# Products with past states in the other quarters of TensorE, fixed PSUM banks, and the low words' top bits on ScalarE

## The chip, the cores and the metric

One core of a Trainium2 chip runs the whole program. The metric is the device time of one execution, in microseconds (us), as the median of several executions. An engine is named as in the profile: PE is TensorE's matmul, PEld its weight load, DVE is VectorE, ACT is ScalarE, POOL is GpSimd, SP is SyncE, which issues nearly all DMAs.

## The reference, cut to what matters

Three layers in a row. The first is a linear recurrence over 768 time steps for 4 batches of 8 heads of width 48; the second a mixture with 32 soft slots; the third a gated MLP whose weights come as float64.

```
for t in range(S):                                    # S = 768
    state = alpha[:, :, t, :, None] * state + k_t (x) v_t
    y[:, :, t] = q_t @ state
x = y as (3072, 384)
logits = x @ phi;  slots = softmax over tokens, x -> 8 experts (relu) -> back to tokens
out = (silu(x @ w_gate) * (x @ w_val)) @ w_out        # float64 weights, float32 result
```

## The kernel before, in words

**Groups.** Two heads sit side by side on the partitions (0 to 47 and 64 to 111). A unit is such a pair for one batch (16 units), and a group is half a unit, that is three chunks of 128 steps: 32 groups, numbered g, with h = 0 for the first half of a unit and h = 1 for the second. The recurrence is done by chunk: `scan_w` and `scan_p` make running products of alpha on VectorE (L307, L314), `scale` multiplies k and q by them on GpSimd (L325), `emit_s` makes the 128x128 score products (L353), `emit_masks` masks them (L360 on VectorE, L362 on ScalarE and L363 on GpSimd), `emit_kt` transposes k (L371, copied out by L374), `emit_dh` makes each chunk's addition to the state (L390), `emit_st` adds the state before it (L402) and scales it on ScalarE (L404), `emit_past` multiplies q by the state before the chunk (L420), and `emit_ip` adds the masked scores times v (L432), after which ScalarE copies the three chunks to `xt` in one instruction (L434). `emit_xt` and `emit_l` transpose `xt` for the slots (L462, copied by L466) and make the logits (L453). After each 8 groups a batch is complete and `slot_steps` puts its steps (`peak`, `exps`, `keep`, `e_tok`, `part`, `l_tok`, `c_norm`) into the groups that follow.

**Order.** The schedule is written by hand: each engine runs its instructions in the order of the program text. In the loop of `fast`, group g issues on PE: state products, scores of g + 1, state products, k transposes of g + 1, `emit_xt` and `emit_l` of g - 1, a slot step, `emit_past(g)`, `emit_dh(g + 1)`, `emit_ip(g)`. A float32 product is two PE instructions with a weight load each.

**Tiles of the array.** `emit_past` has 64 contraction rows and up to 64 output columns for each head: the first head uses rows and columns 0 to 63 of the array, the second 64 to 127. `emit_s` uses the two halves of the rows, `emit_dh` and `emit_ip` the two halves of the columns. PSUM banks come from a pool of three (`psm`, in turn), two for scores, and one each for y and the logits.

**Float64 weights.** A block of `wgv` or `wo` comes as pairs of 32-bit words. For `wgv`, in the loop, `conv_y` scales the high words as float32 on ScalarE (`to_f32_y`, L249) into a place `z_c`; `conv(0)` takes the top three bits of the low words on VectorE (`to_f32_z`, L253); `conv(1)` and `conv(2)` join both and put the sign back on VectorE (`to_f32_p` L257, `to_f32_s` L261). 24 such blocks are converted, one in a group, in 24 of the groups. Each raw block lies in one of two places, and the load of the block after next is issued by SP when `conv_y` and `conv(0)` have read it.

**Memory.** An arena of two areas, near (31600 floats for each partition) and far (19184), holds everything; `pump` loads the slot layer's weight blocks (1536 floats, 768 KB) ahead in it, paced by a credit of 840 floats a group while unit loads remain, into whatever space is free. After the loop come the expert products (L856, L914) and then the MLP (L1010, L1011, L1049).

Of the kernel before, what the change touches and what calls it, by code (L numbers as in the profile page):

```python
# [11 lines left out]
U32 = mybir.dt.uint32  # L12
AF = mybir.ActivationFunctionType
# [21 lines left out]
GV0, RATE = 1, 840  # L35
TINY = 2.0 ** -55
NEAR, ROUND = 31600, 19184
# [55 lines left out]
def attention_slots_mlp(ctx: ExitStack, tc: tile.TileContext, kq, at, vt, phi, w1, w2, wgv, wo, cst, out):  # L93
# [13 lines left out]
    phs = const.tile([112, NU, NSL], F32, name="phs")  # L107
# [6 lines left out]
    amm = const.tile([112, 2, B * NU], F32, name="amm")  # L114

# [25 lines left out]
    def program(general):  # L141
# [14 lines left out]
        z_c = [(ar.alloc(GP, 0), GP)]  # L156

        zn = {nm: [0] * n for nm, n in (("a", 4), ("p", 5), ("v", 4), ("w", 2), ("x", 2))}
        zsize = {"a": HW, "p": HB, "v": 288, "w": HW, "x": 384}
        for z in "a0 a1 p2 a2 p3 v0 w0 a3 p4 v1 w1 p0 v2 p1 v3 x0 x1".split():  # L160
            zn[z[0]][int(z[1])] = ar.alloc(zsize[z[0]], 1)
# [17 lines left out]
        def psm():  # L179
            return ps_m.tile([128, 512], F32, tag="m", name="m")  # L180
# [82 lines left out]
        def done_c():  # L263
            drop(z_c.pop())
            for o in z_g:
                drop((o, 2 * GP))
            few[1] = ar.alloc(few[2], 0)
# [7 lines left out]
        def conv_y():  # L275
            i = gvd[0]
            if i < NG and ("wgv", divmod(i, 4)) in have:
                gvy[i] = to_f32_y(view(have["wgv", divmod(i, 4)]))

        def conv(part):  # L280
            i = gvd[0]
            if i not in gvy:
                return
            n, p = divmod(i, 4)
            raw = view(have["wgv", (n, p)])
            if n not in gvb:
                gvb[n] = need(BLK)
            dst = view((gvb[n][0] + GP * p, GP))
            if part == 0:
                to_f32_z(dst, raw)  # L290
# [11 lines left out]
        def scan_w(g, between=lambda: None):  # L302
# [5 lines left out]
            between()  # L308
# [71 lines left out]

        def emit_dh(g):
# [4 lines left out]
            dps[g] = psm()  # L386
# [4 lines left out]

        dps = {}
# [15 lines left out]
        yps = {}  # L408


        def emit_past(g):
            n, h = sgs[g]
            q = view(qp[g], 112)
            yps[g] = ps_y.tile([128, 512], F32, tag="y", name="y")
            for c in range(3):
                cc = 3 * h + c
                o = slice(c * CH, (c + 1) * CH)
                for s in range(2) if cc else ():
                    p = slice(0, 64) if s == 0 else slice(64, 112)
# [4 lines left out]
        def emit_ip(g):  # L424
            n, h = sgs[g]
            v = view(vv[g]).rearrange("p (c e) -> p c e", e=96)
            ps = yps[g]
            for c in range(3):
                o = slice(c * CH, (c + 1) * CH)
                for s in range(2):  # L430
                    p = slice(0, 64) if s == 0 else slice(64, 112)
                    nc.tensor.matmul(ps[p, o], lhsT=v[:, c, 48 * s:48 * s + p.stop - p.start], rhs=smk[g, s][:, c], start=False, stop=True, skip_group_check=True)  # L432
            xt[g] = (z_x.pop(0), 384)
            nc.scalar.copy(view(xt[g], 112), ps[0:112, 0:384])  # L434
            del smk[g, 0], smk[g, 1], yps[g]
            release(vv.pop(g), z_v, g + 4)
# [8 lines left out]
        def emit_l(g):  # L445
# [5 lines left out]
            for j in range(3):  # L451
                t0 = j * CH
                nc.tensor.matmul(lps[b][32 * j:32 * j + 32, CH * h:CH * h + CH], lhsT=phs[:, u, :], rhs=x[:, t0:t0 + CH], start=(u == 0 and h == 0), stop=(u == NU - 1), skip_group_check=True)  # L453

        def emit_xt(g, between=lambda: None):
# [3 lines left out]
            ps = psm()  # L459
# [8 lines left out]
        def slot_steps(b):  # L468
# [33 lines left out]

            def part(between=lambda: None):
# [3 lines left out]
                for r in range(2):  # L507
                    if r:
                        between()
                    for u, p, w in pieces:  # L510
                        for j in range(3):
                            nc.tensor.matmul(ps[32 * j:32 * j + 32, 96 * u:96 * u + 96 * w], lhsT=st["et"][:, r, 32 * j:32 * j + 32], rhs=xtok[:, p:p + w, 3 * r + j, :], start=(r == 0 and u == 0), stop=(r == 1), skip_group_check=True)
# [64 lines left out]
        def fast():  # L577
            pump_units(4)
# [43 lines left out]
            for g in range(NSG):  # L622
                n, h = sgs[g]
                nxt = g + 1 < NSG

                emit_st(g, 1 - h)
                if GV0 < g and (g <= 8 or g % 8 not in (3, 4)):
                    conv_y()
                if g + 3 < NSG:
                    scan_w(g + 3, lambda: conv(0))  # L630
                    scan_p(g + 3)
                else:
                    conv(0)
# [17 lines left out]
                if g:  # L651
                    emit_l(g - 1)
                    release(xt.pop(g - 1), z_x, g + 1)
# [7 lines left out]
                emit_past(g)  # L661
# [20 lines left out]
                pump_units()  # L682
            for r in z_t:
# [449 lines left out]
def _arrays(q, k, v, alpha, moe_phi, moe_w1, moe_w2, moe2_w_gate, moe2_w_val, moe2_w_out):  # L1133
# [17 lines left out]
    ph = np.zeros((112, NU, NSL), np.float32)  # L1151
    pr = moe_phi.reshape(NU, 2, D, NSL)
    for s in range(2):
        ph[64 * s:64 * s + 48] = pr[:, s].transpose(1, 0, 2)
# [32 lines left out]
```

## Time and profile before

| | |
|---|---|
| median of 3 runs | 388.98 us (387.81 to 390.64) |
| the profiled execution's own time | 387.89 us |
| its span, first to last instruction | 386.2 us |
| mean granted TensorE clock | 0.993 |
| loop over the groups | from about 10 to 153 us of the span |
| expert products | about 158 to 186 us |
| MLP | about 186 to 386 us |
| busy: PE, PEld, DVE, ACT, POOL | 95%, 72%, 76%, 52%, 27% |

The profiled execution lies 1.1 us under the median of the runs. A page's busy share is a mean over the three stages, which have different limits, so a stage is read by its own window. PE's busy time counts the pipeline's length of each matmul, so the pace of PE is read from the distance between starts. SP's rows are issues of DMAs; the time in such a row is the issue alone.

### The profile page before, as it was taken

The page shows a single profiled execution, that of the slowest core. Times are in us where ns is not written, and L with a number is a line of the kernel's source. Part 1 is how long each engine was busy: PE and PEld are TensorE (multiplying, and loading weights), DVE is VectorE, ACT ScalarE, POOL GpSimd, SP SyncE. Part 2 cuts the span into 40 slices and gives each one's busy share as a digit, 9 for nine tenths or more (in the row PEclk, how much of TensorE's full clock was granted, in tenths as well). Part 3 has the DMA queues.
Part 4 walks back from the last instruction along what each step waited for, and adds up shares of the span by engine and source line. Part 5 has one row for each costly group of instructions (what it writes and reads, how often), then busy time and mean ns, then how long its engine had stood idle before and what let it go on. Part 6 is the DMA issues. An engine that isn't in the chain of part 4 may idle for free.

```text
span 386.2 us, 8613 instructions
## 1 busy us (share of the span) xinstructions
PE 368.8 (95%) x3308; PEld 277.0 (72%) x3309; DVE 292.4 (76%) x566; ACT 200.8 (52%) x468; POOL 102.4 (27%) x105
## 2 busy tenths in 40 slices
PE   7799999999999999999899999999999999999992
PEld 3577777776777776433478778888888888888781
DVE  6999899999999973306789977777677867977540
ACT  2366665665567455523467655455445446446441
POOL 3379666795587650011200000000000000000000
PEclk9999999999999999999999999999999999999997
DMA  8999999999899986899900013204204104112002
GB/s 276 354 300 343 374 342 316 321 342 338 281 369 361 304 286 217 345 367 413 351 2 0 3 48 111 68 28 126 74 1 153 50 23 153 38 36 82 3 2 90
DMA packets 28627, 74.25 MB, mean 192 GB/s; under 512 B 3216, under 2 KB 11648, under 8 KB 28576
## 3 DMA queue, kind: packets, MB, share of 16 engines
q1 hardware_dynamic: 28256, 73.27, 53.9%
q8 instruction: 28, 0.46, 0.5%
q10 hardware_dynamic: 272, 0.21, 0.2%
q14 instruction: 23, 0.19, 0.2%
q0 software_dynamic: 48, 0.13, 0.1%
HBM read 68.87 MB, written 4.72 MB: 191 GB/s over the span
## 4 chain that ended last, share of the span: by engine, by line
PE 73%; DVE 6%; DMA 3%; ACT 2%; issue 1%; DVEq 0%; ACTq 0%
PE m L1049 22%; PE acc L1049 11%; PE s L353 4%; PE y L432 4%; PE y L420 4%; PE s L1010 4%; PE s L1011 4%; DMA near<-w 3%; PE s L856 3%; PE m L402 3%; PE m L390 2%; PE m L371 2%; PE l L453 2%; PE m L462 2%; DVE near L1016 2%; DVE rnd L1024 1%
## 5 line engine op out<-in xcount | busy, mean ns | idle before, releaser
L1049 PE MATMUL m<-rnd 128*128 128x512 f32 x432 | 129.3, 389 | 0.0
L1049 PEld LDWEIGHTS m<-rnd 128*128 128x128 f32 x432 | 81.1, 188 | 16.8
L1013 ACT ACTIVATE near<-s 128x512 f32<-128x512 f32 x72 | 43.1, 598 | 79.1 <-PE s L1010 79.1
L1049 PE MATMUL acc<-rnd 128*128 128x512 f32 x216 | 81.1, 392 | 0.8 <-DVE rnd L905 0.8
L325 POOL TENSOR_TENSOR far<-far 112x384 f32<-112x384 f32 x61 | 74.5, 1239 | 9.7 <-DVE far L307 4.7
L1016 DVE TENSOR_TENSOR near<-near,s 128x512 f32<-128x512 f32 x72 | 49.3, 685 | 35.3 <-ACT near L1013 35.3
L1024 DVE TENSOR_TENSOR rnd<-near,rnd 128x512 fp32r<-128x512 f32 x72 | 49.4, 686 | 3.1 <-ACT rnd L1022 3.1
L1049 PEld LDWEIGHTS acc<-rnd 128*128 128x128 f32 x216 | 40.5, 188 | 10.2 <-DVE rnd L905 1.6
L1022 ACT CAST rnd<-near 128x512 fp32r<-128x512 f32 x72 | 44.2, 614 | 0.2 <-DVE near L1016 0.2
L404 ACT ACTIVATE far<-m,tots 112x48 f32<-112x48 f32 x80 | 24.2, 302 | 24.1 <-PE m L402 13.3
L307 DVE TENSOR_TENSOR_SCAN far<-far,r 112x388 f32<-112x388 f32 x32 | 30.8, 961 | 5.8 <-DMA far<-at 3.2
L353 PE MATMUL s<-far 64*128 64x128 f32 x384 | 30.5, 289 | 3.5 <-POOL far L325 3.5
L1120 DVE TENSOR_REDUCE amm<-near 112x1 f32<-112x768 f32 x32 | 30.3, 946 | 3.5 <-DMA near<-at 3.5
L363 POOL TENSOR_SCALAR_AFFINE_SELECT far<-far 128x384 f32<-128x384 f32 x32 | 21.7, 677 | 42.3 <-ACT far L362 42.3
L314 DVE TENSOR_TENSOR_SCAN far<-far,r 112x387 f32<-112x387 f32 x32 | 30.7, 959 | 1.1
L434 ACT COPY far<-y 112x384 f32<-112x384 f32 x32 | 15.3, 479 | 27.7 <-PE y L432 27.7
L353 PEld LDWEIGHTS s<-far 64*128 64x128 f32 x384 | 24.4, 187 | 6.1 <-POOL far L325 4.4
L432 PE MATMUL y<-far 128*48 128x128 f32 (+1 forms) x384 | 28.6, 274 | 0.0
L1010 PE MATMUL s<-rnd 128*128 128x512 f32 x72 | 28.3, 393 | 0.0
L1011 PE MATMUL s<-rnd 128*128 128x512 f32 x72 | 28.2, 391 | 0.0
L257 DVE SCALAR_TENSOR_TENSOR near<-near 128x384 uint32<-128x384 uint32 x36 | 21.3, 593 | 8.5 <-ACT near L249 7.6
L261 DVE SCALAR_TENSOR_TENSOR near<-near 128x384 uint32<-128x384 uint32 x36 | 24.5, 681 | 0.3
(163 smaller groups left out, 489.7 us busy)
## 6 DMA issues: line engine op xcount, KB each, us to landing
near<-w SPq DMA_DIRECT2D x18, 768.0 KB, 7.7
far<-kq SPq DMA_DIRECT2D x32, 384.0 KB, 5.3
far<-w SPq DMA_DIRECT2D x14, 768.0 KB, 5.6
near<-wgv SPq DMA_DIRECT2D x24, 384.0 KB, 5.9
far<-at SPq DMA_DIRECT2D x32, 194.0 KB, 5.2
near<-at SPq DMA_DIRECT2D x16, 339.1 KB, 3.4
far<-vt SPq DMA_DIRECT2D x32, 144.0 KB, 4.7
near<-wo SPq DMA_DIRECT2D x12, 384.0 KB, 7.9
```

Of the source, the lines that this page charges most:

```text
L307: nc.vector.tensor_tensor_scan(w[:, ::-1], a[:, ::-1], rst[:, ::-1], 0.0, ALU.mult, ALU.add)
L314: nc.vector.tensor_tensor_scan(a, a, rst[:, 0:387], 0.0, ALU.mult, ALU.add)
L325: eng.tensor_tensor(out=xv, in0=xv, in1=sv, op=ALU.mult)
L353: nc.tensor.matmul(sps[g][s][:, o:o + CH], lhsT=k[64 * s:64 * s + 64, t0:t0 + CH], rhs=q[64 * s:64 * s + 64, t0:t0 + CH], start=True, stop ...
L432: nc.tensor.matmul(ps[p, o], lhsT=v[:, c, 48 * s:48 * s + p.stop - p.start], rhs=smk[g, s][:, c], start=False, stop=True, skip_group_check ...
L1010: nc.tensor.matmul(pg, lhsT=swk[n][:, 128 * o:128 * o + 128], rhs=ctT[t % 4], start=True, stop=True)
L1011: nc.tensor.matmul(pv, lhsT=swk[n][:, 256 + 128 * o:256 + 128 * o + 128], rhs=ctT[t % 4], start=True, stop=True)
L1013: nc.scalar.activation(sg, pg, AF.Silu)
L1016: nc.vector.tensor_tensor(out=h_, in0=sg, in1=pv, op=ALU.mult)
L1022: nc.scalar.copy(hi, h_)
L1024: nc.vector.tensor_tensor(out=lo, in0=h_, in1=hi, op=ALU.subtract)
L1049: nc.tensor.matmul(p, lhsT=passes[j][0][:, sl], rhs=passes[j][1], start=(f == 0 and j == 0), stop=(f == NF - 1 and j == 2))
```

## The change

- `emit_past` and `emit_ip` swap their order, and `emit_past(g - 1)` moves into group g, behind its first state products. The products with v now open the accumulation, and those with the past state close it; ScalarE's copy to `xt` follows `emit_past`.
- For the middle chunk of a group (`swap`), both put the first head's result on partitions 64 to 111 and the second's on 0 to 63, in another bank. So its products with the past state use the two quarters of the array that the outer chunks leave free. The copy to `xt` becomes two instructions. A second copy of phi with the heads exchanged, and an access pattern that reads the two heads in reverse (`x_rows`), undo the exchange further on.
- In the loop the three pool banks are given out for good: bank 0 for `emit_dh`, bank 1 for `emit_kt`, the slot steps and the middle chunk, bank 2 for `emit_xt`.
- `conv(0)` runs on ScalarE (`to_f32_za`): byte 3 of each low word, divided by 32 and rounded down by a bias. `conv_y` and `conv(0)` move together from the start of a group to the end of the group before, and `z_c` has two places. `wo` keeps the VectorE form.
- `xt` has one place instead of two, the far area is 128 floats smaller, phi's tile 128 larger.

```
-GV0, RATE = 1, 840
+RATE = 840
...
-NEAR, ROUND = 31600, 19184
+NEAR, ROUND = 31600, 19056
...
-        z_c = [(ar.alloc(GP, 0), GP)]
+        z_c = [(ar.alloc(GP, 0), GP), (NEAR - GP, GP)]
...
+        def to_f32_za(dst, raw):
+            nc.scalar.activation(dst.bitcast(U32), raw.bitcast(U8)[:, 3::8], AF.Identity, bias=down, scale=1.0 / 32)
...
+        def y_out(g, s, c):
+            return yps[g][c == 1][half(s ^ swap(c)), CH * (c // 2):CH * (c // 2) + CH]
+        def emit_ip(g):
+            yps[g] = ps_y.tile([128, 512], F32, tag="y", name="y"), mb[1]
+            for c in (0, 2, 1):
+                for s in range(2):
+                    o = y_out(g, s, c)
+                    nc.tensor.matmul(o, lhsT=v[:, e:e + o.shape[0]], rhs=smk[g, s][:, c], start=(c < 2), stop=True, skip_group_check=True)
...
         def emit_past(g):
             for c in range(3):
                 cc = 3 * h + c
                 for s in range(2) if cc else ():
-                    nc.tensor.matmul(yps[g][p, o], lhsT=gst[n, cc][p, 0:p.stop - p.start], rhs=q[p, o], start=(cc == max(1, 3 * h)), stop=False, skip_group_check=True)
+                    o = y_out(g, s, c)
+                    nc.tensor.matmul(o, lhsT=gst[n, cc][half(s), 0:o.shape[0]], rhs=q[half(s), c * CH:(c + 1) * CH], start=False, stop=True, skip_group_check=True)
+            nc.scalar.copy(x[:, CH:2 * CH], z[0:112, 0:CH])
+            nc.scalar.copy(x.rearrange("p (c t) -> p c t", t=CH)[:, 0::2], y[0:112, 0:2 * CH].rearrange("p (c t) -> p c t", t=CH))
...
                 emit_st(g, 1 - h)
-                if GV0 < g and (g <= 8 or g % 8 not in (3, 4)):
-                    conv_y()
+                if g:
+                    emit_past(g - 1)
                 if g + 3 < NSG:
-                    scan_w(g + 3, lambda: conv(0))
+                    scan_w(g + 3)
...
-                emit_past(g)
                 if nxt:
                     emit_dh(g + 1)
...
                 if late:
                     pend.pop(0)()
                     pend.pop(0)()
+                if g <= 7 or g % 8 not in (2, 3):
+                    conv_y()
+                    conv(0)
```

## Rows read from the trace of the kernel before

**Rows 1.** Busy tenths of the DMA engines in 40 slices of the span, from the page.
```profile
DMA  8999999999899986899900013204204104112002
```

**Rows 2.** Timeline of PE over two groups: start us, us, line, operation, tiles, count.
```profile
103.67 0.65 PE L420 MATMUL y<-far 64*64 64x128 f32 x8
...
104.25 0.43 PE L390 MATMUL m<-far 128*64 128x48 f32 x8
...
105.28 0.31 PE L402 MATMUL m<-far,cs 64*64 64x48 f32 x4
...
105.53 0.94 PE L353 MATMUL s<-far 64*128 64x128 f32 x12
...
106.39 0.31 PE L402 MATMUL m<-far,cs 64*64 64x48 f32 x4
...
107.71 0.87 PE L420 MATMUL y<-far 64*64 64x128 f32 x12
...
108.51 0.49 PE L390 MATMUL m<-far 128*64 128x48 f32 x11
...
108.89 0.84 PE L432 MATMUL y<-far 128*64 128x128 f32 x11
109.66 0.31 PE L402 MATMUL m<-far,cs 64*64 64x48 f32 x4
```

**Rows 3.** Busy time of the engines in two stretches: PE, PEld, DVE, ACT, POOL, clock, DMA share, GB/s.
```profile
40.00:45.00 5.00, 5.00 (x81) 3.87 (x78) 4.84 (x12) 3.14 (x9) 3.28 (x4) 1.00 1.01 372
...
60.00:90.00 30.00, 29.42 (x447) 22.92 (x445) 28.59 (x65) 18.82 (x55) 21.31 (x22) 1.00 0.95 328
```

**Rows 4.** Timeline of VectorE around the step that moves.
```profile
105.43 0.33 DVE L253 TENSOR_SCALAR near<-near 128x384 uint32<-128x384 uint32 x1
...
105.68 0.15 DVE L309 TENSOR_TENSOR tots<-far,r 112x3 f32<-112x3 f32 x1
```

**Rows 5.** Groups of ScalarE by line, 60 to 120 us: count, busy us, mean ns, idle before.
```profile
L404 ACT ACTIVATE far<-m,tots 112x48 f32<-112x48 f32 x35 | 10.6, 303 | 9.0 <-PE m L402 4.7 <-PE m L390 4.1
...
L434 ACT COPY far<-y 112x384 f32<-112x384 f32 x14 | 6.7, 478 | 12.0 <-PE y L432 12.0
...
L249 ACT ACTIVATE near<-near 128x384 f32<-128x384 f32 x10 | 5.6, 555 | 0.0
...
L374 ACT COPY far<-m 128x336 f32<-128x336 f32 x7 | 3.1, 439 | 1.2 <-PE m L371 1.2
...
L374 ACT COPY far<-m 128x224 f32<-128x224 f32 x7 | 2.4, 345 | 0.5
```

**Rows 6.** Timeline of PE where a batch ends (group 16).
```profile
87.83 0.31 PE L402 MATMUL m<-far,cs 64*64 64x48 f32 x4 [0.58 <-ACT far L404]
```

**Rows 7.** The same stretch on ScalarE.
```profile
87.23 0.35 ACT L494 COPY lt<-l 96x256 f32<-96x256 f32 x1
87.48 0.30 ACT L404 ACTIVATE far<-m,tots 112x48 f32<-112x48 f32 x1
```

**Rows 8.** Timeline of ScalarE over one group.
```profile
114.29 0.56 ACT L249 ACTIVATE near<-near 128x384 f32<-128x384 f32 x1
...
116.17 0.50 ACT L362 COPY far<-s 128x384 f32<-128x384 f32 x1
117.42 0.30 ACT L404 ACTIVATE far<-m,tots 112x48 f32<-112x48 f32 x1 [0.75 <-PE m L390]
...
118.66 0.56 ACT L249 ACTIVATE near<-near 128x384 f32<-128x384 f32 x1
```

**Rows 9.** Timeline of SP: the issue of a load.
```profile
106.78 0.37 SPq L244 DMA_DIRECT2D near<-wgv  x1
```

**Rows 10.** Line 244's DMAs, all 24: us from issue to landing.
```profile
DMA to landing us min/median/max: 4.3/5.9/8.1
```

**Rows 11.** SP's issues of weight blocks at the loop's end; a row of several has its waits inside.
```profile
137.72 3.88 SPq L236 DMA_DIRECT2D far<-w  x2
```

**Rows 12.** Who waited for whom, 170 to 190 us: total us, times, longest.
```profile
PE so L914 <- DMA near<-w: 1.3, 2, 1.1
```

More of the change, by code (lines that the diff above doesn't have):

```diff
@@ L277, in conv_y @@
             if i < NG and ("wgv", divmod(i, 4)) in have:
-                gvy[i] = to_f32_y(view(have["wgv", divmod(i, 4)]))
+                gvy[i] = to_f32_y(view(have["wgv", divmod(i, 4)]), i % 2)
         def conv(part):
@@ L300, in program, with scan_w @@
         kp, qp, vv, wreg, pair = {}, {}, {}, {}, {}
-        def scan_w(g, between=lambda: None):
+        def scan_w(g):
             n, h = sgs[g]
@@ L406, in emit_st, with swap, half @@
                 del dps[g]
-        yps = {}
+        def swap(c):
+            return int(c == 1 and not general)
+        def half(s):
+            return slice(0, 64) if s == 0 else slice(64, 112)
+        def y_out(g, s, c):
+            return yps[g][c == 1][half(s ^ swap(c)), CH * (c // 2):CH * (c // 2) + CH]
+        def emit_ip(g):
+            yps[g] = ps_y.tile([128, 512], F32, tag="y", name="y"), mb[1]
+            v = view(vv[g])
+            for c in (0, 2, 1):
+                for s in range(2):
+                    o = y_out(g, s, c)
+                    e = 96 * c + 48 * s
+                    nc.tensor.matmul(o, lhsT=v[:, e:e + o.shape[0]], rhs=smk[g, s][:, c], start=(c < 2), stop=True, skip_group_check=True)
+            del smk[g, 0], smk[g, 1]
+            release(vv.pop(g), z_v, g + 4)
         def emit_past(g):
@@ L413, in emit_past @@
             q = view(qp[g], 112)
-            yps[g] = ps_y.tile([128, 512], F32, tag="y", name="y")
             for c in range(3):
                 cc = 3 * h + c
-                o = slice(c * CH, (c + 1) * CH)
                 for s in range(2) if cc else ():
-                    p = slice(0, 64) if s == 0 else slice(64, 112)
-                    nc.tensor.matmul(yps[g][p, o], lhsT=gst[n, cc][p, 0:p.stop - p.start], rhs=q[p, o], start=(cc == max(1, 3 * h)), stop=False, skip_group_check=True)
+                    o = y_out(g, s, c)
+                    nc.tensor.matmul(o, lhsT=gst[n, cc][half(s), 0:o.shape[0]], rhs=q[half(s), c * CH:(c + 1) * CH], start=False, stop=True, skip_group_check=True)
+            xt[g] = (z_x.pop(0), 384)
+            x = view(xt[g], 112)
+            y, z = yps.pop(g)
+            nc.scalar.copy(x[:, CH:2 * CH], z[0:112, 0:CH])
+            nc.scalar.copy(x.rearrange("p (c t) -> p c t", t=CH)[:, 0::2], y[0:112, 0:2 * CH].rearrange("p (c t) -> p c t", t=CH))
             del qp[g]
             release(pair.pop(g), z_p, g + 5)
[L424 to L436, printed above, removed]
         def release(r, z, g):
@@ L452, in emit_l @@
                 t0 = j * CH
[L453 removed]
+                nc.tensor.matmul(lps[b][32 * j:32 * j + 32, CH * h:CH * h + CH], lhsT=phs[:, swap(j), u, :], rhs=x[:, t0:t0 + CH], start=(u == 0 and h == 0), stop=(u == NU - 1), skip_group_check=True)
         def emit_xt(g, between=lambda: None):
@@ L577, in fast @@
         def fast():
+            mb.extend([psm() for _ in range(3)])
             pump_units(4)
@@ L682, in fast @@
                 pump_units()
+            emit_past(NSG - 1)
+            mb.clear()
             for r in z_t:
```

47 lines of the change are left out of this document (30 added, 17 removed).

## The prediction

> **What bounds the kernel now.** I read the table of times first, then the strip of the page, then windows, then timelines of single groups. The change lies in the loop over the groups, so its stage decides. The strip [rows 1] shows the DMA engines near full up to 135 us, with a dip in three slices (135 to 164 us, around the loop's end), then full again to 193 us and nearly idle in the MLP. The window 60 to 90 us [rows 3] has VectorE busy for 28.59 of 30 us and the DMA engines at 0.95 with 328 GB/s; 40 to 45 us has them at 1.01 with 372 GB/s. PE's busy figure says little, its starts do: from 105.28 to 109.66 us each group of products follows the one before at the distance that its own count asks for [rows 2], and nothing in it is marked as a wait. So PE, VectorE and the loads all run close to their limits in the loop, at 4.0 us (L420 to L420) to 4.4 us (L402 to L402) a group, 4.2 in the middle. PE sets the pace, VectorE has 5% left and the loads have 5% or nothing. What a shorter PE group is worth depends on which of the other two is met first.
>
> **PE.** Eight instructions of `emit_past` take from 103.67 to 104.25 us, 0.58 us to the next kind; twelve take from 107.71 to 108.51, 0.80 us [rows 2]. Four instructions more, which is one chunk with two heads, thus cost 0.22 us, and 0.58 - 2 x 0.22 = 0.14 us is paid once, for entering this shape. The two heads of a chunk share these 0.22 us, since they lie in different quarters. After the change the middle chunk shares them with another chunk (with chunk 0 where h = 1, with chunk 2 where h = 0, as the first chunk of a unit has no past): 0.22 us less in every group. Moving it behind the state products (L402, same 64x64 shape) saves up to the 0.14 us of entry; I take 0.10, as the scores behind it still have theirs. `emit_ip` issues the same twelve instructions. That is 0.32 us a group. Groups 0 to 2 wait for the first loads, so 29 groups count: 29 x 0.32 = 9.3 us, the most that PE can give. Both ends of the price: 29 x 0.22 = 6.4 us without the entry, and 29 x 0.10 = 2.9 us if the quarters do not overlap.
>
> Whether quarters that share rows overlap is not in the trace, but halves are. The products of L432 use every row and one half of the columns each; from 108.89 to 109.66 us [rows 2] they start 0.07 us apart. Taking turns they would be 0.11 us apart, the time in which two instructions of `emit_past` stream the same 128 columns side by side. So column halves over the same rows run at once, each with its own moving data, and I take it that four quarters do.
>
> Against this the Trainium skill, "TensorE: Matmul & The Clock Gate", Part 3 (Packing small matmuls), says that a weight load overlaps matmuls in flight only when it goes to another group of rows. By that rule the middle chunk's products would wait for the outer chunk's on the same rows, and of the 9.3 us only the 2.9 us of the entry would be left. The rows of L432 do not agree with it, so it gets a small chance below.
>
> **VectorE.** `conv(0)` leaves it. The next instruction starts 0.25 us later, and its own time is 0.33 us [rows 4]. Ten conversions fall into 60 us [rows 5], five into 30 us: 1.25 to 1.65 us less in 30 us, and of the 1.4 us that are free [rows 3] some may be used. Over the 128 us of the loop in which the engines are full (25 to 153 us) that allows 5.4 to 7.0 us without the free share, up to 13 with all of it; I take 8. VectorE is not the first limit, but near it.
>
> **ScalarE.** The trace has no byte-reading instruction. The nearest row is `conv_y`, 555 ns for the same 384 elements at the same stride; a per-partition operand, which the new bias is, costs 303 ns at 48 columns (L404) against 345 - 176 x 0.84 = 197 ns for a copy of 48, with 0.84 ns a column from the two forms of L374 [rows 5]. So 555 + 106 = 660 ns is my estimate; VectorE's 0.33 us and twice `conv_y`, 1.1 us, are the ends. The split copy: 128 columns 264 ns and 256 columns 372 ns by the same line, 636 against 478 ns. In 30 us that is 5 x 0.66 + 7 x 0.16 = 4.4 us on top of 18.82 [rows 3], so 23.2 of 30: by busy time off the path. What costs is the order. The conversion is now ahead of the next state scaling in ScalarE's queue.
> - In an ordinary group PE needs the scaled state 1.1 us after its first state products (105.28 to 106.39 us [rows 2]), 1.5 us with `emit_past` between. `conv_y` would start when L362 or L404 ends (116.67 or 117.72 us [rows 8], 0.9 to 2.0 us before the place where it starts now), so 1.2 us of conversion is over in time. I cost it at nothing; PE's scores and `emit_past` hide it, and without that cover it costs up to 1.2 us a group.
> - At a batch's end PE already waits: 0.58 us at group 16 [rows 6], for a ScalarE queue that ends with `keep` at 87.23 us and the scaling at 87.48 us [rows 7]. Behind `keep` now come `conv_y` and the new step, some 1.0 us, less 0.25 us that VectorE is earlier with the maximum. I take 0.8 us more for each of groups 8, 16 and 24: 2.4 us. Ends: 0 and 3.6.
> PE's share is then 9.3 - 2.4 = 6.9 us.
>
> **Loads.** Faster groups ask for the same bytes in less time. At full share the window of 60 to 90 us would give 328 / 0.95 = 345 GB/s, 5.2% more; 5.2% of 128 us is 6.7 us. Groups 3 to 8 (30 to 55 us, 25 us) are full already, which takes 1.3 us off: 5.4 us. This is the lowest of the three limits. Where it bites is `conv_y`: the load issued at 106.78 us [rows 9] is used two groups later at 114.29 us [rows 8], 7.5 us; afterwards two groups are 0.64 us shorter, `conv_y` comes 0.9 to 2.0 us earlier (less 0.3 us, as ScalarE's other work moves back), and SP issues it some 0.4 us later, as the k and q load ahead of it now waits for the `emit_past` of the next group. 4.8 to 5.9 us are left for landings of 4.3 to 8.1 us, median 5.9 [rows 10]. ScalarE will often wait there, with the scaling, the copies to `xt` and so PE behind it; PE notices when the wait passes 0.5 to 1 us. I put the loop at 5.2 us saved, the loads' 5.4 with a little of that wait, from 0 to 9.3.
>
> **After the loop.** Far space: one `xt` place less and 128 floats less area make 256 more free floats. From the sizes in the code 5896 floats are free beside the loop's zones before, 3 weight blocks, and 6152 after, 4 blocks and 8 floats; near holds 19 blocks in both cases (29680 and 29296 floats). So one block more can be loaded before the loop's zones come free, where SP now waits (two issues take 3.88 us at 137.72 us [rows 11]) and the DMA engines have their dip [rows 1]. That takes 0.77 MB from the full stretch behind it. PE's waits for weight blocks there are 1.3 us [rows 12], which bounds the gain; nothing is the other bound, if PE's use of w1 releases the space as late as now. I take 1.0 us. The MLP is untouched.
>
> **Sum.** 387.89 - 5.2 - 1.0 = 381.7 us for the profiled execution. Runs spread by 0.4% and their median is 1.1 us higher, so I forecast 382.8 us. A difference under 1% (3.9 us) is about what a measurement of this kernel cannot tell from none.
>
> **The rivals.**
> - *PE's whole gain comes through*: 9.3 + 1.3 us, 378.4 us. For it: lookahead is two groups and ScalarE's idle time could swallow late landings. Against it: VectorE at 95% and the loads' 5%. Chance 0.14.
> - *The loads give nothing*: `conv_y`'s wait holds PE at the present pace in most groups, only the slot groups and the loop's last four gain, 2 us, with 0.5 after the loop: 386.5 us. For it: 372 GB/s at full share early on. Chance 0.20.
> - *The quarters go in pairs*: 2.9 us of PE less 2.4 at the batches' ends, 1.0 after: 387.5 us. Against it: L432. Chance 0.08. This is also the case in which the change does not do what it says.
> - *Slower*: the load's way to `conv_y` becomes the loop's period. From the spacing above, two groups then last the landing plus 1.8 to 2.9 us, less PE's patience of some 0.75 us: (landing + 1.6) / 2 for one group, in the middle. That equals the 4.2 us of now at a landing of 6.8 us, and from there on groups are longer than now; at 8.1 us it is 4.85 us. If 12 of the 24 converting groups are so, they cost 12 x 0.65 = 7.8 us, the batches' ends 2.4; 1.0 after the loop and 17 other groups with 0.2 us each give 4.4 back: 5.8 us more, 394.8 us. For it: landings up to 8.1 us. Against it: the median of 5.9, and a longer group also gives the loads time. Chance 0.12.
> - *The forecast*: 380.5 to 385.1 us, chance 0.46.
>
> **How the numbers follow.** The range, 377.5 to 389 us, holds all but the slower case and the outer parts of the others. Faster by over 1% (under 385.1): 0.14 and nearly all of 0.46, 0.60. Within 1%: 0.20, 0.08 and a rest, 0.29. Slower: 0.11.
>
> **What the profile will show.** Right: `emit_past` with twelve instructions in about 0.6 us to the scores; no L253 on VectorE in the loop; an ACTIVATE of bytes of about 0.66 us; a seventeenth weight block issued without a wait where the last v load goes out; the loop ending near 148 us. The wait to look for is ScalarE's on `wgv`, and PE's on L404's successor. Wrong: twelve instructions still in 0.8 us; ScalarE's byte step over 1.1 us; PE waiting for bank 1 behind a slot step's VectorE copy; the granted clock falling in the loop from its 1.00.

## The result and the profile after

The change takes 383.56 us (median of 4 runs, 382.91 to 385.54) against 388.82 us before on the same chip (median of 4, 387.81 to 390.64). The ratio is 0.9878, 95% interval 0.9839 to 0.9916: 1.2% faster. Medians here are of all executions; a ratio is estimated by itself and without the few disturbed executions, so it is not quite the quotient of two medians. The profiled execution took 384.14 us with a span of 382.4 us, against 387.89 and 386.2 us before.

Line numbers have moved: the state products are L417 (L402 before), their scaling on ScalarE L419 (L404), `emit_past` L453 (L420), `emit_ip` L442 (L432), `conv_y` L260 (L249), the scores L368 (L353), the copies to `xt` L457 and L458 (L434), the expert products L890 and L948 (L856, L914). L265 is the new byte step.

First the page's strips. The DMA strip answers to [rows 1]; the clock strip is PE's granted clock in tenths.

```profile
PEclk9879999999999999999999999999999999999997
DMA  8979999999899998899600014113104204112002
```

The dip around the loop's end is nearly gone. The second and third clock digits, 8 and 7, are new and come back below. Next PE over one group and a part of the next, answering to [rows 2] (start, duration, line, operation, count).

```profile
103.47 0.25 PE L417 MATMUL m<-far,cs 64*64 64x48 f32 x2
103.48 0.33 PE L453 MATMUL m<-far 64*48 64x128 f32 x2
...
103.60 0.31 PE L453 MATMUL y<-far 48*48 48x128 f32 x2
...
103.71 0.30 PE L453 MATMUL y<-far 48*48 48x128 f32 x2
103.94 0.94 PE L368 MATMUL s<-far 64*128 64x128 f32 x12
...
107.29 0.25 PE L417 MATMUL m<-far,cs 64*64 64x48 f32 x2
...
107.53 0.52 PE L453 MATMUL y<-far 48*48 48x128 f32 x6
107.99 0.94 PE L368 MATMUL s<-far 64*128 64x128 f32 x12
```

State products and past products now start among each other, bank m beside bank y. From the first state product to the scores it is 0.47 us where eight past products lie between and 0.70 us where twelve do. Before, the same work was 0.25 us (105.28 to 105.53) and 0.58 or 0.80 us [rows 2], 0.83 and 1.05 us in sum: 0.36 and 0.35 us less.

The windows answer to [rows 3] (PE, PEld, DVE, ACT, POOL, clock, DMA share, GB/s).

```profile
40.00:45.00 5.00, 4.64 (x72) 3.51 (x69) 4.80 (x11) 3.74 (x13) 2.65 (x4) 1.00 1.03 399
60.00:90.00 30.00, 28.83 (x479) 21.92 (x476) 27.07 (x62) 22.81 (x72) 17.11 (x22) 1.00 0.96 343
```

In 60 to 90 us VectorE falls from 28.59 to 27.07, ScalarE rises from 18.82 to 22.81, GpSimd falls from 21.31 to 17.11, and the loads move 343 in place of 328 GB/s. Early on the loads stand at 1.03 and 399 GB/s.

A mean over such a stretch hides one thing, since eight of the 32 groups convert nothing. In an ordinary group that converts, VectorE goes from one instruction to the next with gaps of 0.09 us at most, and by the starts of its first scan (L307 before, L323 after) such a group took it 4.40 us before (68.63 to 73.04 us) and takes 3.91 us now (72.85 to 76.76 us).

ScalarE's groups from 60 to 120 us answer to [rows 5] (count, busy us, mean ns, idle before and what ended it).

```profile
L265 ACT ACTIVATE near<-near,down 128x384 uint32<-128x384 uint8 x10 | 6.5, 645 | 0.0
...
L260 ACT ACTIVATE near<-near 128x384 f32<-128x384 f32 x10 | 5.6, 561 | 3.0 <-DVE tots L324 1.6 <-DMA near<-wgv 1.2 <-DVE near L276 0.3
L458 ACT COPY far<-y 112x256 f32<-112x256 f32 x14 | 5.4, 385 | 0.1
L457 ACT COPY far<-m 112x128 f32<-112x128 f32 x14 | 3.7, 263 | 0.0
```

`conv_y`, which did not wait in this stretch before, now waits 3.0 us in it. For 1.6 us VectorE's row stands there as the releaser that came last by the profile, but `conv_y` reads nothing of it. That wait ends at 116.93 us, the load landed at 116.56 us, and 1.19 of its 1.55 us lie ahead of the landing; what held the rest is not shown. One such wait on ScalarE, and PE behind it:

```profile
111.79 0.57 ACT L260 ACTIVATE near<-near 128x384 f32<-128x384 f32 x1 [1.17 <-DMA near<-wgv]
112.26 0.64 ACT L265 ACTIVATE near<-near,down 128x384 uint32<-128x384 uint8 x1
112.79 0.29 ACT L419 ACTIVATE far<-m,tots 112x48 f32<-112x48 f32 x1
```

```profile
111.58 0.94 PE L368 MATMUL s<-far 64*128 64x128 f32 x12
113.14 0.31 PE L417 MATMUL m<-far,cs 64*64 64x48 f32 x4 [0.62 <-ACT far L419]
```

The loads themselves are as quick as before: 5.6 us in the median to landing, against 5.9 [rows 10]. They are asked for later against their use, as `conv_y` has moved up: in ordinary groups where it hardly waits, 5.3 to 5.6 us lie between issue and use (30.49, 34.15 and 80.31 us), where it was 7.5 us.

To see where the time went I took from both traces the start of the first product with v (L432, L442) of each group and measured between them:

```
                              before   change   same kernel again
first L442 of group 2           24.2     26.2     23.4
group 2 to group 31            127.9    122.5    124.1
group 31 to expert products      7.9      8.4      8.4
expert products to the end     226.2    225.3    225.3
ordinary groups, one       3.97/4.34  3.80/3.84  3.80/3.84
groups 8, 16, 24 to the next   5.59 5.31 5.31   4.38 5.22 4.80   4.38 5.24 4.81
```

The loop gives 5.4 us and the part behind it 0.9; 2.0 us are lost ahead of group 2, and 0.5 in the third line (`emit_past` of the last group now lies behind that mark). The third column is a second execution, told below.

At the loop's end SP's issues answer to [rows 11] and PE's waits for weight blocks from 157 to 190 us to [rows 12] (total us, times, longest).

```profile
135.15 0.33 SPq L232 DMA_DIRECT2D far<-vt  x1
135.53 0.42 SPq L247 DMA_DIRECT2D near<-w  x1
136.11 1.13 SPq L247 DMA_DIRECT2D far<-w  x1
```

```profile
PEld so L948 <- DMA near<-w: 1.3, 2, 1.1
...
PE so L948 <- DMA near<-w: 0.4, 1, 0.4
```

Behind the last v load (L232) two blocks go out within 1.7 us; before, one was issued and the second waited within the 3.88 us. The DMA share from 135 to 150 us rises from 0.76 to 0.88, and PE's own wait falls from 1.3 to 0.4 us.

### The profile page after: what moved, and what is told of

Same layout as the page of the kernel before. It is cut to its first block, busy times and chain, and to the rows that moved or that the text cites. A ratio compares the mean times of both kernels' runs of the same rounds, so it can differ in the third digit from the quotient of the medians.

```text
span 382.4 us, 8742 instructions
## 1 busy us (share of the span) xinstructions
PE 362.6 (95%) x3309; PEld 269.3 (70%) x3309; DVE 283.9 (74%) x543; ACT 214.3 (56%) x524; POOL 84.8 (22%) x105
## 4 chain that ended last, share of the span: by engine, by line
PE 50%; DVE 8%; DMA 2%; ACT 2%; issue 1%; DVEq 0%; ACTq 0%
PE m L1083 22%; PE acc L1083 11%; PE s L1044 4%; PE s L1045 4%; PE s L890 3%; DMA near<-w 2%; DVE near L1050 1%; DVE rnd L1058 1%; PE sw L1013 1%; DVE near L804 1%; DVE rnd L939 1%; DVE near L276 1%; PE s L368 1%; PE m L808 1%; DVE near L272 0%
## 5 line engine op out<-in xcount | busy, mean ns | idle before, releaser
L340 POOL TENSOR_TENSOR far<-far 112x384 f32<-112x384 f32 x61 | 60.6, 1013 | 8.8 <-DVE far L323 4.5
L419 ACT ACTIVATE far<-m,tots 112x48 f32<-112x48 f32 x80 | 23.9, 299 | 28.2 <-PE m L417 26.0
L323 DVE TENSOR_TENSOR_SCAN far<-far,r 112x388 f32<-112x388 f32 x32 | 30.8, 962 | 6.3 <-DMA far<-at 3.7
L368 PE MATMUL s<-far 64*128 64x128 f32 x384 | 30.8, 293 | 3.3 <-POOL far L340 2.0
L368 PEld LDWEIGHTS s<-far 64*128 64x128 f32 x384 | 24.7, 191 | 9.4 <-issue 4.8
L378 POOL TENSOR_SCALAR_AFFINE_SELECT far<-far 128x384 f32<-128x384 f32 x32 | 17.6, 550 | 59.0 <-ACT far L377 59.0
L272 DVE SCALAR_TENSOR_TENSOR near<-near 128x384 uint32<-128x384 uint32 x36 | 20.2, 562 | 9.3 <-ACT near L265 5.4
L417 PE MATMUL m<-far,cs 64*64 64x48 f32 (+1 forms) x256 | 20.2, 232 | 5.2 <-ACT far L419 4.8
L260 ACT ACTIVATE near<-near 128x384 f32<-128x384 f32 x36 | 20.2, 563 | 6.3 <-DMA near<-wgv 2.4
L417 PEld LDWEIGHTS m<-far,cs 64*64 64x64 f32 (+1 forms) x256 | 12.2, 126 | 15.9 <-ACT far L419 7.5
```

The source lines that it names most:

```text
L323: nc.vector.tensor_tensor_scan(w[:, ::-1], a[:, ::-1], rst[:, ::-1], 0.0, ALU.mult, ALU.add)
L340: eng.tensor_tensor(out=xv, in0=xv, in1=sv, op=ALU.mult)
L368: nc.tensor.matmul(sps[g][s][:, o:o + CH], lhsT=k[64 * s:64 * s + 64, t0:t0 + CH], rhs=q[64 * s:64 * s + 64, t0:t0 + CH], start=True, stop ...
L417: nc.tensor.matmul(dps[g][p, c * 48:c * 48 + 48], lhsT=ident[p, p], rhs=gst[n, cc - 1][p, 0:48], start=False, stop=True, skip_group_check= ...
```

## The experiments

The theory to be tested: the middle chunk in the other quarters gives 0.22 us a group, its place behind the state products about 0.10; VectorE is relieved by the byte step; the load that `conv_y` waits for takes part of it back. The rivals are that quarters on the same rows take turns, that the gain is VectorE's alone, and that the loads' wait is what holds the loop. Each kernel below is the changed kernel with the edits named, and was run beside the kernel before on the same chip (its median: 387.81, 388.22 and 388.23 us in the three sets). The change itself was run again in the first set, with the next three kernels; the later ones ran on two other chips and are compared with it by way of the kernel before.

**The change again.** No edit.

> The changed kernel once more, on the chip of the three runs beside it, as their point of comparison. Both theories: a ratio to the kernel before of 0.985 to 0.990 (383 to 385 us). Theory 1 (PE's loop is shorter by some 0.33 us a group, and half of it is lost to waits that the conversion's new place makes, and to a low TensorE clock in group 1) expects in the profile: ScalarE idle before line 260 for 1 us or more in 3 to 6 groups, PE idle behind it, and a granted clock of 0.5 somewhere between 14 and 25 us. Theory 2 (the low clock was chance in one profiled execution) expects the clock at 1.00 there.

Measured 383.63 us (381.13 to 387.06), ratio 0.989, 0.9837 to 0.9943. The gain stands. In this execution the granted clock was 1.00 from 14 to 26 us and group 2 came at 23.4 us; the loop took 124.1 us, with longer waits for the loads (PE waits of 1.65 us at 37 us and 1.58 us at 115 us; here and below a wait of PE is counted from the start of one product to the start of the next, while a mark in brackets counts from the end of the first, 0.27 us less).

**Without the other quarters.**

```
-            return int(c == 1 and not general)
+            return 0
```

> The middle chunk keeps its quarters (swap gives 0); order, banks and conversion stay as changed. Theory 1: emit_past's twelve instructions take 0.65 to 0.70 us to the scores instead of 0.44 to 0.51, 0.22 us more in each group; groups that wait for ScalarE anyway (about 9 of 31) hide it, so 20 x 0.22 = 4 to 5 us slower than the change. Rival (VectorE or the loads set the loop's pace): under 1.5 us slower, although the products take longer.

Measured 385.89 us (12 runs, 384.88 to 387.79), ratio 0.9942, 0.9914 to 0.9969: 2.3 us slower than the change, between the two expectations. The intervals touch, but seven of the change's ten executions lie under the lowest of these. PE from the state products to the scores, in the group that has eight past products:

```profile
103.79 0.31 PE L417 MATMUL m<-far,cs 64*64 64x48 f32 x4
103.92 0.41 PE L453 MATMUL m<-far 48*48 48x128 f32 x4
104.15 0.41 PE L453 MATMUL y<-far 48*48 48x128 f32 x4
104.49 0.94 PE L368 MATMUL s<-far 64*128 64x128 f32 x12
```

That is 0.70 us against 0.47 us with the quarters, and the ordinary groups are 4.02 and 4.06 us apart in place of 3.80 and 3.84: 0.22 us a group for the quarters. From 4.155 us, the mean of before, to 4.04 us is 0.115 us for the rest of the change. The next run keeps 3.80 and 3.84 us without the conversion's part, so this is the order and the fixed banks, which no run takes apart. The rival that quarters take turns falls. Over 29 groups 0.22 us would be 6.4 us, but only 2.3 us are lost: the change itself waits longer for the loads (3.0 us in its trace, 1.8 us in this one) and in the groups behind the batches' ends (this kernel is 1.5 us longer there, where twelve shares would be 2.6), so most of what PE gains by the quarters is given back there.

**The conversion where it was, on VectorE.**

```
-                to_f32_za(dst, raw)
+                to_f32_z(dst, raw)
...
+                if 1 < g and (g <= 8 or g % 8 not in (3, 4)):
+                    conv_y()
...
+                    scan_w(g + 3, lambda: conv(0))
...
-                if g <= 7 or g % 8 not in (2, 3):
-                    conv_y()
-                    conv(0)
```

> The conversion goes back to the start of the group, behind emit_past, and the low words' top bits go back to VectorE between its scans; products, order and banks stay as changed. Theory 1: ScalarE no longer waits for the loads of wgv and PE's waits for ScalarE (6 to 7 us in the loop) fall under 2 us; VectorE gets 24 x 0.25 = 6 us more work and becomes the loop's limit at about 4.2 us in a converting group, so within 2 us of the change either way. Rival (VectorE's relief is what made the loop shorter): 4 to 6 us slower than the change, close to the kernel before.

Measured 386.30 us (12 runs, 385.35 to 389.19), ratio 0.9962, 0.9929 to 0.9994: 2.7 us slower than the change, again between the two expectations; the same seven executions of the change lie under the lowest. The profiled execution, 388.70 us, is one of the slowest of the twelve. Its ordinary groups are 3.80 and 3.84 us apart all the same, although VectorE needs 4.29 us for one that converts (73.97 to 78.25 us between starts of L323): PE runs ahead, and the difference is paid at the batches' ends. Groups 8, 16 and 24 take 5.09, 6.17 and 7.18 us in place of 4.38, 5.22 and 4.80, and ScalarE there waits for VectorE's maximum of the logits (2.5 us at most); behind the last of them the clock is at 0.50 from 125.2 to 128.6 us. GpSimd's products of alpha with k and q, 60 to 90 us, first this kernel, then the change:

```profile
L341 POOL TENSOR_TENSOR far<-far 112x384 f32<-112x384 f32 x15 | 20.2, 1362 | 0.0
```

```profile
L340 POOL TENSOR_TENSOR far<-far 112x384 f32<-112x384 f32 x15 | 14.7, 999 | 0.0
```

The same instruction takes 1362 ns where VectorE also has the low words (1281 ns in the kernel before), 999 ns where it hasn't. So the quarters and the conversion's move bring about as much each. This edit moves the conversion back both to its engine and to its place, and does not tell the two apart.

**A warm start.** Six idle products on PE in group 1 (`keep_warm(6, mb[2])` behind `emit_past`), bfloat16 products of the tile of constants (identity and mask) with itself, whose result nobody reads, because the clock was at 0.50 from 17 to 23 us in the change's profile.

> Six matmuls without use are put on PE behind emit_past(0), into bank 2, where PE waits 2.3 us for GpSimd in group 1. Theory 1: the clock stays at 1.00 and group 1 ends near 20.9 us instead of 22.7; 1.8 us faster than the change in those executions in which the clock fell, 1 to 2 us in the median. Rival (the low clock was chance, or the loads of group 2 end at the same time anyway): under 0.5 us.

Measured 383.68 us, ratio 0.9898, 0.9860 to 0.9936: no gain in the median. The low clock at the start is not in every execution (it wasn't in the second of the change), and the medians show no cost of it.

**The weights' load issued earlier.** The raw place counts as free when the byte step has read it, and the next load goes out in the middle of the group.

```
                 to_f32_za(dst, raw)
+                z_g.append(have.pop(("wgv", (n, p)))[0])
...
                     del kp[g + 1]
+                    pump_gv()
```

> A raw wgv place is given back when ScalarE has read it twice (it was held until the sign step), and the load for it is issued in the middle of the group, ahead of the k and q load instead of behind the alpha load. Theory 1 (part of PE's waits comes from conv_y waiting for its load): loads go out some 1 us earlier and with 0.6 MB less ahead of them, ScalarE's idle time before line 260 on DMA goes to under 0.5 us, PE's waits of 1 us or more away from the batch ends vanish, 2 to 3 us faster than the change. Rival (the loads as a whole are the limit): the wait moves to other loads (k and q, alpha), under 1 us.

Measured 387.10 us (12 runs, 385.76 to 390.05), ratio 0.9978, 0.9947 to 1.0008: 3.5 us slower than the change, against what was expected. The waits of `conv_y` are gone, from group 2 on, and the ordinary groups run at 3.80 and 3.84 us (but for one of 4.21), while groups 8 and 24 take 6.40 and 6.54 us. VectorE and ScalarE at the end of the first batch:

```profile
48.66 0.53 DVE L272 SCALAR_TENSOR_TENSOR near<-near 128x384 uint32<-128x384 uint32 x1
49.11 0.55 DVE L374 TENSOR_TENSOR far<-s,cs 128x384 f32<-128x384 f32 x1
49.58 0.41 DVE L502 TENSOR_REDUCE nmx<-l 96x1 f32<-96x256 f32 x1
```

```profile
50.02 0.47 ACT L511 ACTIVATE e<-l,nmx 96x256 f32<-96x256 f32 x1 [1.45 <-DVE nmx L502]
```

ScalarE waits 1.45 us for the maximum (L502), and VectorE reaches it without a gap: it is the late one. In the change the same place reads

```profile
49.32 0.55 DVE L375 TENSOR_TENSOR far<-s,cs 128x384 f32<-128x384 f32 x1
50.29 0.42 DVE L503 TENSOR_REDUCE nmx<-l 96x1 f32<-96x256 f32 x1 [0.42 <-PE l L477]
```

where VectorE waits 0.42 us for PE's logits. VectorE's converting group takes 3.91 us here too (42.46 to 46.37 us between starts of the scan, L322), PE's 3.82 us. So, as far as these rows tell, the waits for the loads in the change hold PE back to about VectorE's place; take them away, and PE runs ahead and pays at the batch's end in one piece, 1.69 us at 50.4 us and 2.41 us at 120.6 us. And there is a second cost. The stretches behind the first of these waits:

```profile
51.00:52.00 1.00, 0.00 (x0) 0.00 (x0) 0.94 (x1) 1.00 (x4) 0.67 (x1) 1.00 1.06 394
52.00:53.00 1.00, 0.94 (x10) 0.77 (x10) 0.90 (x4) 0.82 (x5) 0.00 (x0) 0.99 0.56 170
53.00:54.00 1.00, 1.00 (x10) 0.48 (x8) 1.00 (x3) 1.00 (x3) 0.00 (x0) 0.50 0.77 207
...
55.00:56.00 1.00, 1.00 (x12) 0.90 (x9) 0.90 (x3) 0.95 (x3) 1.00 (x2) 0.50 0.70 231
```

PE idles a whole microsecond, runs again, and from 53 to 56.4 us the granted clock is 0.50 (1.2 GHz); the same follows the wait at 120.6 us, from 124.7 to 128 us.

**No conversion at the batch's end.** The groups of eight that skip it are those with index 0 and 3 in place of 2 and 3.

```
-                if g <= 7 or g % 8 not in (2, 3):
+                if g <= 7 or g % 8 not in (0, 3):
```

> The two groups of eight that convert nothing are now those whose index leaves 0 and 3 (they left 2 and 3), so that no conversion stands behind exps and keep at a batch's end. Theory 1: PE's waits of 0.9 to 1.3 us behind groups 16 and 24 shrink to 0.3 us, and no more than four conversions follow one another there, so fewer late loads: 2 us faster than the change. Rival (VectorE in the slot groups sets the pace, and the conversion in group 2 of 8 now lands on it): no gain, or up to 1 us slower.

Measured 383.35 us, ratio 0.9865, 0.9816 to 0.9915: the same as the change. Groups 8, 16 and 24 go down to 4.12, 4.25 and 4.25 us, but PE waits 1.0, 1.2 and 1.1 us for ScalarE at 46, 76 and 115 us instead. What is saved at one place is waited at another.

**Both edits together** (the early load and the skipped ends).

> Both of the two edits above. Theory 1: the sum, 3 to 5 us faster than the change (378.5 to 380.5 us), at which the loop runs at PE's 3.82 us in every group without a slot step. Rival (loads or VectorE): 1 us or less.

Measured 382.99 us, ratio 0.9856, 0.9809 to 0.9903: not to be told from the change.

**One far block less.** The far area 16 floats smaller, so that three weight blocks fit beside the loop's zones and not four.

```
-NEAR, ROUND = 31600, 19056
+NEAR, ROUND = 31600, 19040
```

> The far area is 16 floats smaller (19040), so that three weight blocks fit beside the loop's zones instead of four; nothing else changes. Theory 1 (the fourth block is worth PE's waits on weight loads after the loop, 1.0 us in the prediction): 0.5 to 1.3 us slower than the change, and the last w2 block lands later against the loop's end. Rival (PE's use of w1 paces the loads): no difference above 0.4 us.

Measured 385.27 us (12 runs, 382.85 to 391.59), ratio 0.9902, 0.9869 to 0.9934. That is 1.7 us over the change, while the intervals overlap. The profile bears the mechanism out: the DMA share from 135 to 150 us is 0.73 (0.88 with the fourth block), and PE's waits for weight blocks from 157 to 190 us are 1.9 us (0.4). From the expert products to the end it takes 227.4 us, where the eleven other traces on the changed kernel, all with the fourth block, take 224.9 to 226.0. This execution also had the longest wait for a load behind group 2, ScalarE 2.24 us, PE 1.93 us (1.66 by its mark):

```profile
110.49 0.55 ACT L260 ACTIVATE near<-near 128x384 f32<-128x384 f32 x1 [2.24 <-DMA near<-wgv]
```

```profile
111.80 0.31 PE L417 MATMUL m<-far,cs 64*64 64x48 f32 x4 [1.66 <-ACT far L419]
```

and again the clock is at 0.50 behind it (from 112.7 to 116.1 us).

**Early load, and idle products in the wait.** The same six idle products on PE in groups 9, 17 and 25, ahead of the state products that wait. (The expectations call them products of zeros; what they read is the tile of constants.)

```
                         emit_s(g + 1, c)
+                if g in (9, 17, 25):
+                    keep_warm(6, mb[2])
                 emit_st(g, 2 - h)
```

> The kernel with the early loads of the weights (wgv_early), and six products of zeros on PE in groups 9, 17 and 25, between the scores and the state products at which PE waited 1.69, 1.29 and 2.41 us. Six such products took 1.4 us in an earlier run, so they lie inside the wait and delay nothing by more than 0.1 us. Theory A (a PE wait of 1.5 us and more is paid twice, once as the wait and once as the 0.50 of the granted clock that followed it for 3.4 us, at 53 and at 124.6 us): the clock stays at 1.00 there, groups 9 and 25 take some 5.5 us in place of 7.2 and 7.3, and the time falls from 387.1 to about 384 us. Theory B (the early loads cost time by their place in the order of the loads, and the clock is incidental): no change, about 387 us.

Measured 383.27 us (6 runs, 382.74 to 387.05), ratio 0.9866, 0.9822 to 0.9910; its interval lies clear of that of the early load alone (0.9947 to 1.0008). Theory A holds by the medians: products that compute nothing bring back 3.8 us. The two kernels ran on different chips, each beside the kernel before, so this rests on the ratios. The mean granted clock of the runs is 0.985 to 0.996, against 0.974 to 0.987 without them. In the profiled execution the clock is 1.00 behind the ends, the first of them here:

```profile
52.00:54.00 2.00, 1.97 (x14) 0.90 (x13) 1.80 (x6) 2.00 (x8) 1.16 (x1) 1.00 0.77 283
54.00:56.00 2.00, 2.00 (x34) 1.49 (x32) 2.00 (x4) 1.54 (x5) 0.41 (x1) 1.00 0.84 254
```

The expected lengths of the end groups don't show there, though: this execution was the slowest of its six, and VectorE came so late that groups 8, 16 and 24 took 5.80, 6.46 and 7.01 us at full clock. The gain is thus shown in the medians and the clocks, not in the length of a group.

**Early load, the maximum ahead of VectorE's conversion step** in groups 8, 16 and 24 (`conv(1)` moved behind `peak`).

> The kernel with the early loads, and in groups 8, 16 and 24 VectorE takes the maximum of the logits before its own step of the conversion instead of after it, so the maximum comes about 0.45 us earlier. Theory A (with the loads in time, VectorE's queue sets the wait at a batch's end, since ScalarE waited 1.45 and 1.82 us for that maximum): the PE waits at the ends fall by about 0.45 us each, 1.4 us in all, and more if one of the falls of the clock goes with them: 383 to 386 us. Theory B (ScalarE's own queue sets it, conversion included): the waits stay, 387 us.

Measured 385.18 us (11 runs, 381.67 to 389.61), ratio 0.9892, 0.9855 to 0.9929: 1.9 us better than the early load alone, and the interval lies just clear of that one's. In the profiled execution, one of the slowest of its eleven (387.56 us), ScalarE's wait for the maximum at the first batch falls from 1.45 to 0.99 us, the 0.46 us by which the maximum moved:

```profile
49.94 0.53 DVE L374 TENSOR_TENSOR far<-s,cs 128x384 f32<-128x384 f32 x1
50.38 0.41 DVE L502 TENSOR_REDUCE nmx<-l 96x1 f32<-96x256 f32 x1
```

```profile
50.83 0.47 ACT L511 ACTIVATE e<-l,nmx 96x256 f32<-96x256 f32 x1 [0.99 <-DVE nmx L502]
```

VectorE still runs without a gap into it, so its queue sets that wait, as theory A has it.

**All three together.**

> Early loads, the maximum before the conversion step, and the products of zeros, all three. If each cause is what it seems, the gains add: waits of about 1.3, 0.9 and 1.9 us at the ends, the clock at 1.00 through the loop, and 382 to 383 us, as good as the change or 1 us better. If the loop's pace is set by VectorE's total work, nothing is left to gain against the change and it comes out at 383 to 384 us.

Measured 383.42 us (6 runs, 382.83 to 385.16), ratio 0.9869, 0.9825 to 0.9913. That is the change's own time, as was expected if VectorE's work is the limit; its converting groups take 3.91 us here too, and groups 8, 16 and 24 still take 5.52, 5.52 and 6.39 us. No version beats the change by more than its interval.

## Why the prediction was right

The forecast, 382.8 us, lies 0.8 us from the median. What it said of PE, of ScalarE's step, of the loads' wait and of the part after the loop is what the runs show; the loss that it put at the batches' ends has nearly its size by another cause, and VectorE stood nearer than it said. By its steps:

**PE, 0.32 us a group.** Measured 0.335 us between ordinary groups (4.155 to 3.82 us). Its two terms come apart in the run without the quarters: 0.22 us for the quarters, as forecast, and 0.115 us for the order with the fixed banks, taken as 0.10. The inference from the column halves of L432 held. The rule of the Trainium skill ("TensorE: Matmul & The Clock Gate", Part 3), by which a weight load overlaps matmuls in flight only on another group of rows, is not what this trace shows: with all four quarters in use, 0.47 us against 0.70 us for the same eight products.

**ScalarE.** The byte step took 645 ns, estimated 660; the split copy 263 + 385 = 648 ns, estimated 636. In an ordinary group without a late load this cost PE nothing, as said.

**The batches' ends, 2.4 us.** Near in size, but not by the cause given. Groups 8, 16 and 24 with the three behind each took 57.9 us before and 55.6 us after (sums of the twelve distances), 2.3 us less, where twelve times 0.335 us would be 4.0: 1.7 us were lost, not 2.4. The cause given was the conversion behind `keep`, ahead of the scaling that PE waits for. It is there at group 16, where PE's wait by its mark goes from 0.58 us [rows 6] to 1.03 us, but against ordinary groups of their kind (4.34 and 3.80 us) groups 8, 16 and 24 together were 3.2 us longer before and are 3.0 us longer now: nothing is lost in the three. The loss lies further back. Groups 11, 19 and 27 take 4.26 us, where they took an ordinary 3.97 us and the ordinary is now 3.84, 1.3 us in all; most of the other 0.4 lies in groups 18 and 26. There PE waits for bank 1, which the middle chunk shares with the slot steps. Group 11, PE and then ScalarE:

```profile
64.19 0.62 PE L442 MATMUL y<-far 128*64 128x128 f32 x7
64.78 0.44 PE L442 MATMUL m<-far 128*48 128x128 f32 x4
65.37 0.25 PE L417 MATMUL m<-far,cs 64*64 64x48 f32 x2
```

```profile
64.76 0.36 ACT L561 ACTIVATE ct<-ct 128x192 f32<-128x192 f32 x1 [0.64 <-DVE ct L560]
65.03 0.28 ACT L419 ACTIVATE far<-m,tots 112x48 f32<-112x48 f32 x1
```

The middle chunk's products (bank m) start 0.59 us after the first of the row above them, and only 0.36 us after in an ordinary group (106.53 to 106.89 us). They start when VectorE's step L560 of `l_tok`, which reads bank 1, ends at 64.73 us; ScalarE's step behind it then makes the scaled state late as well, and PE starts L417 at 65.37 us. Before, `emit_past` stood between the slot step and these products. This is one of the prediction's own signs of being wrong, PE waiting for bank 1 behind a slot step on VectorE. The sum came near by luck here. No run gave the slot steps another bank, so what that would bring is open.

**The loads, 5.4 us as the lowest limit.** The place was right: `conv_y` waits, then the scaling, then PE. In the profiled execution four ordinary groups are longer than 3.8 us by 0.4, 0.9, 0.7 and 1.1 us, 3.0 us in all. PE's 29 x 0.335 = 9.7 us, less 1.7 and 3.0, plus 0.4 from the loop's last group, is the 5.4 us that the loop shows, forecast 5.2. What the prediction had too simple is the ranking. It let PE set the pace before and put VectorE's limit at 8 us, from a busy share that also holds groups without a conversion. By its starts VectorE was the slower engine in a converting group before (4.40 us against PE's 4.155) and is so after (3.91 against 3.82); PE ran ahead of it, and the difference was made up in the groups that convert nothing and at the batches' ends. So the loads and VectorE lie side by side: with the loads in time, in the early load, VectorE's queue holds PE up at the ends and nothing is won.

**GpSimd** was not in the sum. It runs faster beside a relieved VectorE (21.31 to 17.11 us busy in 60 to 90 us), and no run shows whether that gave time by itself.

**After the loop, 1.0 us.** From the expert products to the end 0.9 us, with the fourth far block in the place that the prediction named; without it that part is 2.1 us longer in the trace, while the 1.7 us in the medians are not clear of the noise.

**What it missed.** Ahead of group 2 the profiled execution lost 2.0 us, of which nothing was forecast; the loop ended later than the 148 us that it named for this reason. With it the granted clock fell in the loop, at group 1, which was another of its signs of being wrong. In the second execution that loss isn't there, and the loop gives 3.8 us only, by longer waits for the loads. So the median holds sums that change places from run to run, and the hit to 0.8 us is in part luck. The slower rival had the right place but not the price: landings stayed at a median of 5.6 us, under the 6.8 us from which it would have decided. PE's whole gain didn't come through for the loads and VectorE, and the loads' wait took a third of it, not nearly all.

## What to carry to other kernels

Where three limits lie within a few per cent of each other, cost a faster engine by the next limit, not by its own saving: here 9.7 us on PE were worth 5.4 in the loop. And removing the wait that is seen can only show the next one, at a worse place: many waits of under a microsecond were cheaper than one long wait, behind which PE's clock fell as well. An engine's limit is read from its own period in the groups that are full, as the mean busy share over all groups hid VectorE's 4.40 us. And a bank that is given a second user makes a wait where the first is late. Matmuls on separate quarters with separate banks are worth trying wherever small products stand in turn on the same half of the array.

## What was not expected of the hardware

**The granted clock inside a busy loop.** It fell to 0.50 (1.2 GHz) for some microseconds after PE had idled. In the change's own profile this is at the start, where PE waited from 14.74 to 17.02 us for GpSimd's scaled k and q:

```profile
14.00:16.00 2.00, 1.01 (x22) 0.59 (x17) 1.81 (x5) 0.73 (x3) 1.20 (x2) 1.00 1.02 392
16.00:18.00 2.00, 0.98 (x8) 1.01 (x10) 1.90 (x4) 0.00 (x0) 1.01 (x2) 0.64 0.88 303
18.00:20.00 2.00, 2.00 (x16) 1.69 (x15) 1.85 (x6) 0.32 (x2) 0.00 (x0) 0.50 0.97 326
20.00:22.00 2.00, 2.00 (x26) 1.34 (x26) 1.85 (x4) 1.31 (x4) 0.67 (x2) 0.50 0.81 313
22.00:24.00 2.00, 2.00 (x29) 1.50 (x26) 1.23 (x2) 1.57 (x5) 1.64 (x2) 0.66 0.13 52
```

Further inside the loop it followed PE waits of 1.48 (the two edits together, at 120 us), 1.49 (the conversion on VectorE, at 123 us), 1.69, 1.93, 2.11 (the maximum ahead, at 123 us) and 2.41 us, but not waits of 1.65 and 1.58 us in the second execution of the change. At the start it followed a wait of 2.3 us in the change, the conversion on VectorE, and three of the runs with the early load, but not the same wait in the run with all three and the run without a conversion at the batch's end, nor 2.4 us at 14.4 us in the kernel before. What decides between these stays open. The spread of one kernel's runs goes with the mean granted clock in part: the change took 381.1 us at 0.998 and 387.1 us at 0.978, but 382.91 us at 0.986 and 382.99 us at 0.997.

**GpSimd and VectorE.** The same GpSimd product took 999 ns in the change and 1362 ns with the low words back on VectorE, both means of 60 to 90 us. Which of VectorE's instructions lengthens it is not shown.
